# A four-segment memory attention and GEGLU layer on one core: masked keys written by small copies into zeroed tiles, free choice of PSUM pairs, and a replanned order

## The chip, the cores and the metric

One Trainium2 chip, one core of it. The metric is the device time of one execution in microseconds (us), lower is better. The kernel before takes 561.71 us, the median of three runs (561.22 to 561.72). Its engines are named as in the profile: PE multiplies matrices, PEld loads its weights, DVE and ACT and POOL work on tiles in SBUF (the on-chip memory) and in PSUM (eight banks, into which PE writes), SP issues nearly all DMAs.

## The reference, cut to what matters

The input has 2048 rows of 512. Two layers are applied twice with the same weights: an attention A and a gated feed-forward block B, each behind a layer norm and each added to its input.

```python
for s in range(4):                       # four segments of 512 rows, 32 heads of 16
    logits = einsum(qs, ks) * scale + mask          # causal inside the segment
    a_dot = softmax(logits) @ vs
    a_mem = (phi(qs) @ M) / (phi(qs) @ z + 1e-6)    # phi(t) = t+1 if t>0 else exp(t)
    o = g * a_mem + (1 - g) * a_dot
    M, z = M + phi(ks).T @ vs, z + phi(ks).sum()    # handed to the next segment
x = x + concat(o) @ wo
x = x + (gelu(n(x) @ w_gate) * (n(x) @ w_up)) @ w_down
```

All tensors are bf16; both layers run twice over the four segments, so that there are eight attention stages and eight feed-forward stages, numbered k = 0 to 7.

## The kernel before, in words

**Planner.** The program is written out by a planner in Python, `order`. It keeps a clock for each engine (`Clocks`, `Engine`), decides at each moment which piece of PE work comes next, and emits the instructions of all five engines in the order thus found. On the chip each engine runs its own instructions strictly in that order and waits at semaphores; the planned times are not there any more. An `Item` is a piece of PE work with a due number in stages (`k - qk_due` for the query and key products of stage k, and so on) and a readiness test; `Engine.post` queues work for another engine with a slack, and the job with the smallest ready time plus slack comes first. The numbers in `POLICY` are these due numbers, slacks and limits.

**Work of a stage.** `qk` and `v` make the products for queries, keys and values, each a chain of four 512-column matmuls into one PSUM bank, which DVE or ACT evicts (`evict`, L366 and L367). Queries, keys and masked keys are tiles of 4 blocks b by 512; a block holds eight heads in 128 partitions. Scores go in 40 rounds a stage (`score_round`, L793): four matmuls side by side, on four row groups of PE. A row group holds 32 partitions, two heads. For the first head of a pair (par = 0) the matmul takes the upper 16 rows of the key tile `kf` and of q. For the second (par = 1) it takes all 32 rows of `kB`, a copy of the keys with the first head's rows set to zero. `kB` comes from POOL: after a key block is evicted, `k_done` (L539) posts a multiplication of the block by `maskB`, a column of zeros and ones. `score` takes two rounds at a time into two pairs of banks, one `exp` of 128x1024 on ACT for each pair (L1199), then a causal mask on POOL (L1205), and later a flush (L809): the product with the values, turned and normalised on DVE (L824, L828, L832, L839).

**Pairs of banks.** In the kernel before a pair is banks 2p and 2p+1, read through the view `ps_pairs`. `pick` gives other work a bank whose neighbour is in use, if there is one, so that whole pairs stay free; `cap` limits how many pairs other work may have.

**Memory part.** `phi` takes exp on ACT (L596), min with 1 (L614, on DVE for stage 0, on POOL after), and add on DVE (L600); for keys the result is turned by a DMA transpose (`turn_later`, L342), `phik`. The rows of the norm, `xn` (L435, DVE), are turned in the same way into `xnT`, for the attention stages and most of the feed-forward ones. The scale `rs` of a norm is made on POOL (L418, L423).

**PE modes.** A matmul is done whole (128 weight columns), or in four column strips of 32 beside each other (`product`, L376 and L379), or, for scores, in row groups. Going from one form to another costs time on PE, which the planner counts as `SWITCH`. Where PE has nothing ready, the planner emits products of the constant tile `warm`, here called fillers.

**Queue of SP.** Loads of inputs and weights, transposes and stores are all issued by SP in one order. Weight pieces are posted with an earliest planned time, but on the chip SP issues them as soon as those ahead of them are issued. Stage 0 keeps its q, kf and kB in space of `wd_sb`, which is loaded later.

Of the kernel before, what the change touches and what calls it, by code (L numbers as in the profile page):

```python
# [18 lines left out]
P = 128  # L19
# [35 lines left out]
    flush_wait=-1.813, piece_slack=1.086, kb_slack=2.08, mem_slack=-2.073, margin=1.389, qk_due=0.513,  # L55
    e_q=-0.257, e_k=1.032, exp_slack=0.902, e_slack=10.959, phi_slack=4.283, gelu_slack=1.187, act_evict=3.627,
    first_evict=4.817, gate_step=0.01, up_due=0.388, up_step=0.027, down_due=2.499, down_step=0.058,
    upd_due=-0.151, v0_due=-1.527, x1_at=10.541, x2_at=16.065, x3_at=40.015, cut_slack=6.049, direct=1,
    gelu_tiles=3, kb_dve=0, phi_pool=1, rounds=2, early=1, starve=0.518, cap=4, fuse=1)


class Engine:
# [4 lines left out]
    def __init__(self, overlap=0.0):  # L67
        self.free, self.overlap, self.jobs, self.table = 0.0, overlap, [], "exp"
        self.only = None
# [17 lines left out]
    def serve(self, now):  # L87

        self.jobs = [j for j in self.jobs if not j[4]]
        jobs = [j for j in self.jobs if not self.only or j[3] in (None, self.only)]  # L90
        if not jobs:
            return False
        start = max(self.free, min(j[0] for j in jobs) + self.LATENCY)
        if start > now:
            return False
        job = min((j for j in jobs if j[0] + self.LATENCY <= start + 0.03), key=lambda j: j[0] + j[1])
        ready, _, steps, table, taken = job
        taken.append(1)
        self.jobs.remove(job)
        t = ready  # L100
        if table and table != self.table:
            self.free += 1.28
            self.table = table
        for cost, emit, told in steps:
            t = max(self.free, t + self.LATENCY) + cost
            self.free = t - self.overlap
            if emit:
                emit()
            if told:
                told(t)  # L110
        return True


class Clocks:
# [6 lines left out]
    def __init__(self):  # L121
        self.pe = 0.0
        self.mode = "whole"
        self.act, self.dve, self.pool, self.sp = Engine(0.09), Engine(0.07), Engine(), Engine()
        self.engines = (self.dve, self.act, self.pool, self.sp)
        self.later, self.seq, self.waiting = [], 0, []
        self.dma, self.fills, self.stalls = 0.0, [], []
        self.ev = {}
# [103 lines left out]
def order(pol, nc, cst, seg, wrk, psp, A_x, A_wq, A_wk, A_wv, A_wo, A_beta, B_x, B_w_gate, B_w_up, B_w_down, out):  # L232
# [34 lines left out]
    pieces = [(14.0, 512, lambda: load_x(2)), (27.0, 512, lambda: load_x(3))]  # L267
# [17 lines left out]
    nc.vector.memset(warm[:], 1.0)  # L285

    ps_all = psp.tile([P, BANKS, L], F32, tag="ps", bufs=1, name="ps")
    ps_pairs = ps_all[:].rearrange("p (a b) c -> p a (b c)", b=2)
# [20 lines left out]
    maskB = cst.tile([P, 1], F32, name="maskB")  # L309
    nc.vector.reduce_sum(out=maskB[:], in_=bd[:, 16:P:32], axis=mybir.AxisListType.X)  # L310
# [81 lines left out]
    class Norm:  # L392
# [46 lines left out]
        def row(self, j, i, ready):  # L439
            xn = Box(lambda: self.normed(j, i))  # L440

            def landed(t):
                xn_slots.back(i, t)
                self.left -= 1
                if not self.left:
                    ev[self.key] = t

            def told(t):
                if self.key in BY_PE:
                    items.append(self.turn_item(j, xn, t, landed))  # L450
# [4 lines left out]
            ck.dve.post(ready, self.slack, (0.46, xn, told))  # L455
# [34 lines left out]
    class Att:  # L490
# [12 lines left out]
        def add_items(self):  # L503
# [5 lines left out]
            def first():  # L509
                if k:  # L510
                    self.q, self.kf, self.kB = (seg.tile([P, KT, L], BF16, tag=f"{n}{k % SETS}", bufs=1, name=n)
                                                for n in ("q", "kf", "kB"))
# [22 lines left out]
            def k_done(b, ps, at=None):  # L535
                def told(t):
                    ev["k", k, b] = t
                    eng, job, cost = (nc.vector, ck.dve, 0.345) if k < pol.kb_dve else (nc.gpsimd, ck.pool, 1.566)
                    job.post(t, pol.kb_slack if k else NORMAL, (cost, lambda: eng.tensor_scalar(  # L539
                        out=self.kB[:, b, :], in0=self.kf[:, b, :], scalar1=maskB[:, 0:1], scalar2=None,  # L540
                        op0=ALU.mult), lambda t2: ev.update({("kB", k, b): t2})))
# [13 lines left out]
            def v(j):  # L555
# [4 lines left out]
                def done():  # L560
# [6 lines left out]
                            lambda: ck.has(("xnTa", k)) and (k <= SETS or ("flush", k - SETS, 3, 1) in ev),  # L567
# [17 lines left out]
        def phi(self, b, which, ready, slack):  # L585
            def take(i):
# [29 lines left out]
                def summed(t):  # L616
                    ck.dve.post(t, pol.phi_slack, (0.75 if which == "q" else 0.83, add, told))

                def made(t):
                    if self.k < pol.phi_pool:  # L620
                        ck.dve.post(t, pol.phi_slack, (0.32, cut(nc.vector), None),
                                    (0.75 if which == "q" else 0.83, add, told))
                    else:
                        ck.pool.post(t, pol.cut_slack, (1.566, cut(nc.gpsimd), summed))
# [154 lines left out]
        def score_round(self, t, places):  # L779
# [5 lines left out]
            for ki, q0, n, c0 in PIECES[i]:  # L785
                for j in range(4):
# [6 lines left out]
                    nc.tensor.matmul(ps_all[:, 2 * pair + unit // 2, o:o + n], lhsT=lhsT[rows, b, P * ki:P * ki + P],  # L793
# [3 lines left out]
        def flush_item(self, b, par, places, masked):  # L797
# [16 lines left out]
            def done():  # L814
# [35 lines left out]
                def put():  # L850
                    steps = [(0.706, back, None if self.s else there)]
                    if self.s:
                        steps.append((0.447, add, there))
# [3 lines left out]
                if par:  # L857
                    steps += [(0.355, inverse, None), (0.7, scale, kept)]
# [185 lines left out]
    first_scale(2, 4)  # L1044
    n0.first_xn = [n0.normed(0, 0), n0.normed(1, 1)]
# [24 lines left out]
    ck.pe, ck.act.free, ck.dve.free, ck.pool.free, ck.sp.free = 8.8, 9.45, 8.9, 6.2, 7.2  # L1070
# [4 lines left out]
    later_constants()  # L1075
    for at, kb, piece in pieces:
# [12 lines left out]
    norm_of_input(1, pol.x1_at, 0.5)  # L1089
    norm_of_input(2, pol.x2_at, 1.0)  # L1090
    norm_of_input(3, pol.x3_at, 1.0)
# [4 lines left out]
    score_pairs = set()  # L1096
# [14 lines left out]
    def free(bank, t):  # L1111
        return banks[bank] <= t
# [7 lines left out]
    def rounds_now():  # L1120

        if not streams:
            return 0
        ready = 0
        for k, t in streams[:pol.rounds]:
            if not att[k].score_ready(t):
                break
            ready += 1
        n = min(len(free_pairs()), len(slot_free), ready)
        if n >= 3 and len(streams) != 4:  # L1130
            return 3
        if n >= 2 and len(streams) != 3 and (streams[0][0] < pol.early or len(streams) in (2, 4) or backlog() < pol.starve):
# [3 lines left out]
    def pick():  # L1136

        got = [i for i in range(BANKS) if free(i, ck.pe)]
        mine = len({i // 2 for i in range(BANKS) if banks[i] > ck.pe and i // 2 not in score_pairs})
        half = [i for i in got if not free(i ^ 1, ck.pe)]  # L1140
        if half:
            return min(half, key=lambda i: (-banks[i ^ 1], banks[i]))
        if got and (mine < pol.cap or not streams):
            return max(got, key=lambda i: i)
        return None
# [8 lines left out]
    def score(n):  # L1154
        pairs = free_pairs()[:n]
# [26 lines left out]
        groups = [[p] for p in range(n)] if n == 2 or not pol.fuse else [[2], [0, 1]] if pol.fuse == 1 else [[0, 1], [2]]  # L1182
        for group in groups:
            jobs, parts = [], []
            for p in group:
                pair, slot = pairs[p], slots[p][1]
                score_pairs.add(pair)
                slot_users[slot] = len(users[p])
                banks[2 * pair] = banks[2 * pair + 1] = 1e9
# [8 lines left out]
            def exp(p0=p0, p1=p1, s0=s0, s1=s1):  # L1198
                nc.scalar.activation(  # L1199
                    out=pt_all[:, s0:s1 + 1:max(s1 - s0, 1), :, :].rearrange("p s u c -> p s (u c)"),  # L1200
                    in_=ps_pairs[:, p0:p1 + 1:max(p1 - p0, 1), :], func=ACT.Exp, scale=SCALE)
# [6 lines left out]
            def told(a, parts=parts, jobs=jobs):  # L1208
                for pair, _ in parts:
                    score_pairs.discard(pair)  # L1210
                    banks[2 * pair] = banks[2 * pair + 1] = a
# [19 lines left out]
    while streams or items or opened or ck.busy():  # L1231
# [16 lines left out]
        if bank is not None:  # L1248
# [6 lines left out]

            if streams:
# [65 lines left out]
```

## Time and profile before

| what | value |
|---|---|
| median of the runs | 561.71 us |
| the profiled execution, its own time | 561.81 us |
| its span on the core | 560.1 us |
| busy share of PE, DVE, ACT, POOL | 97%, 80%, 81%, 58% |
| granted clock of PE | full in all 40 slices |
| kB on POOL (L539), 32 instructions | 46.5 and 6.8 us |
| min with 1 on POOL (L614), 44 instructions | 66.9 us |
| causal masks on POOL (L1205), 320 instructions | 184.1 us |
| exp on ACT (L1199), 320 instructions | 309.7 us |
| packets of DMA queue q1 | 20.1% of 16 engines' span |

Busy time of an engine is the time in which one of its instructions ran. A matmul's recorded time is its way through PE, longer than the distance to the next one, so that a long row of matmuls is priced by its whole length divided by its count. An idle time is put down to the instruction that released it.

### The profile page before, as it was taken

To read this page: it belongs to the slowest core of one execution; us is meant where nothing else is said; L and a number is where in the kernel's file an instruction comes from. 1 tells how busy PE (TensorE), PEld (TensorE's weight loads), DVE (VectorE), ACT (ScalarE), POOL (GpSimd) and SP (SyncE) were. 2 spreads that over 40 slices of the span, in tenths; PEclk is the share of its full clock that TensorE was granted. 3 is DMA by queue.
4 is the path that set the end of the run, shared out by engine and by line. 5 is a ranking of instruction groups with operands and counts; after the bars stand their busy time and mean duration, and the time that the engine had idled before them with its cause. 6 is when DMAs were issued, how large, how long until landed. Compare 5 with 4: busy or idle time off the path is not lost.

```text
span 560.1 us, 21158 instructions
## 1 busy us (share of the span) xinstructions
PE 542.6 (97%) x9193; PEld 271.0 (48%) x9234; DVE 449.8 (80%) x821; ACT 450.9 (81%) x533; POOL 323.8 (58%) x438
## 2 busy tenths in 40 slices
PE   7999999999999999999999999999999999999997
PEld 3444454444445444444444444445445445555544
DVE  4999899979998699789698887988976877886332
ACT  5899999999798978999999699998899986730230
POOL 3699899278724997258881389835785344200000
PEclk9999999999999999999999999999999999999999
DMA  7155801600231023400321030210310004100001
GB/s 225 32 117 169 180 2 31 180 2 2 40 68 12 3 30 61 64 2 12 49 40 22 20 59 4 48 23 12 57 43 22 2 3 78 40 3 21 19 1 37
DMA packets 64925, 25.76 MB, mean 46 GB/s; under 512 B 54336, under 2 KB 64832, under 8 KB 64832
## 3 DMA queue, kind: packets, MB, share of 16 engines
q1 hardware_dynamic: 64400, 24.13, 20.1%
q8 instruction: 72, 1.18, 0.9%
q10 hardware_dynamic: 432, 0.27, 0.2%
q14 instruction: 21, 0.17, 0.1%
HBM read 9.71 MB, written 2.10 MB: 21 GB/s over the span
## 4 chain that ended last, share of the span: by engine, by line
PE 69%; DVE 20%; DMA 4%; issue 3%; ACT 2%; POOL 1%; SPq 0%; ACTq 0%; DVEq 0%
PE ps L376 37%; PE ps L379 19%; PE ps L793 6%; PE ps L809 4%; DVE st L405 3%; DVE xn L435 3%; DVE x_sb L879 2%; DVE byq L824 2%; DMA phik<-e 2%; ACT pt L1199 2%; DVE gel_sb L366 1%; DVE ab L832 1%; DMA wv_sb<-in_A_wv_dram 1%; DVE phiq L600 1%; PE ps L665 1%
## 5 line engine op out<-in xcount | busy, mean ns | idle before, releaser
L1199 ACT ACTIVATE pt<-ps 128x1024 bf16<-128x1024 f32 x320 | 309.7, 1026 | 36.3 <-PE ps L793 32.4
L1205 POOL TENSOR_SCALAR_AFFINE_SELECT pt<-pt 128x512 bf16<-128x512 bf16 (+1 forms) x320 | 184.1, 589 | 132.5 <-ACT pt L1199 131.7
L939 DVE TENSOR_TENSOR gel_sb<-gel_sb,ps 128x512 bf16<-128x512 bf16 x112 | 74.5, 683 | 28.4 <-PE ps L379 17.1
L376 PE MATMUL ps<-wd_sb,gel_sb 128*32 128x512 bf16 (+1 forms) x1296 | 75.2, 370 | 0.0
L614 POOL TENSOR_SCALAR e<-e 128x512 bf16<-128x512 bf16 x44 | 66.9, 1520 | 5.8 <-ACT e L596 4.5
L879 DVE TENSOR_TENSOR x_sb<-x_sb,ps 128x512 bf16<-128x512 bf16 (+1 forms) x68 | 43.2, 645 | 30.9 <-PE ps L376 17.0
L376 PE MATMUL ps<-xnT,wg_sb 128*32 128x512 bf16 x1056 | 64.4, 380 | 0.6 <-DVE gel_sb L366 0.4
L376 PE MATMUL ps<-xnT,wu_sb 128*32 128x512 bf16 x1128 | 64.8, 379 | 0.0
L824 DVE STREAM_TRANSPOSE byq<-ps 128x512 f32<-128x512 f32 x64 | 45.1, 706 | 13.4 <-PE ps L809 12.9
L539 POOL TENSOR_SCALAR kB<-kf,maskB 128x512 bf16<-128x512 bf16 x28 | 46.5, 1661 | 8.5 <-DVE kf L366 8.0
L366 DVE CAST gel_sb<-ps 128x512 bf16<-128x512 f32 x57 | 38.1, 680 | 12.8 <-PE ps L376 5.9
L376 PEld LDWEIGHTS <-gel_sb 128*32 128x32 bf16 x1296 | 32.8, 96 | 29.2 <-issue 5.6
L376 PEld LDWEIGHTS <-wu_sb 128*32 128x32 bf16 x1128 | 30.3, 97 | 28.6 <-issue 2.4
L991 ACT ACTIVATE gel_sb<-gel_sb 128x1536 bf16<-128x1536 bf16 (+1 forms) x35 | 43.4, 1304 | 0.1
L379 PE MATMUL ps<-xnT,wg_sb 128*128 128x512 bf16 x170 | 41.9, 379 | 1.1 <-issue 0.5
L809 PE MATMUL ps<-pt,vaug 128*32 128x256 bf16 (+1 forms) x1344 | 40.8, 256 | 0.0
L405 DVE BATCH_NORM_STATS2 st<-x_sb 128x6 f32<-128x512 bf16 x60 | 40.5, 675 | 0.4
L376 PEld LDWEIGHTS <-wg_sb 128*32 128x32 bf16 x1056 | 27.1, 96 | 26.1 <-issue 5.7
L379 PE MATMUL ps<-xnT,wu_sb 128*128 128x512 bf16 x157 | 37.1, 379 | 0.8 <-issue 0.5
L435 DVE TENSOR_SCALAR xn<-x_sb,mv,rs 128x512 bf16<-128x512 bf16 x64 | 34.2, 592 | 2.7 <-POOL rs L423 2.2
L809 PEld LDWEIGHTS <-vaug 128*32 128x32 bf16 x1344 | 30.5, 97 | 11.4 <-issue 3.9
L793 PE MATMUL ps<-q,kf 16*128 16x256 bf16 (+1 forms) x672 | 31.1, 255 | 1.9 <-ACT pt L1199 1.3
(129 smaller groups left out, 757.2 us busy)
## 6 DMA issues: line engine op xcount, KB each, us to landing
wg_sb<-in_B_w_gate_dram SPq DMA_DIRECT2D x8, 224.0 KB, 5.1
wu_sb<-in_B_w_up_dram SPq DMA_DIRECT2D x8, 224.0 KB, 4.4
wd_sb<-in_B_w_down_dram SPq DMA_DIRECT2D x7, 256.0 KB, 3.1
x_sb<-in_A_x_dram SPq DMA_DIRECT2D x3, 512.0 KB, 6.8
out_dram<-x_sb SPq DMA_DIRECT2D x12, 128.0 KB, 1.7
xnT<-xn SPq DMA_TRANSPOSE x48, 2.5
wv_sb<-in_A_wv_dram SPq DMA_DIRECT2D x1, 512.0 KB, 6.9
wo_sb<-in_A_wo_dram SPq DMA_DIRECT2D x4, 128.0 KB, 3.0
```

The source lines that it names most:

```text
L376: nc.tensor.matmul(out[r], lhsT=lhsT[:, r], rhs=rhs, start=start, stop=stop, tile_position=(0, 32 * c))
L379: nc.tensor.matmul(out, lhsT=lhsT, rhs=rhs, start=start, stop=stop)
L405: nc.vector.bn_stats(out=self.st6[:, 0, :], in_=x_sb[:, self.tt0 + j, :])
L435: nc.vector.tensor_scalar(out=xn[:], in0=x_sb[:, self.tt0 + j, :], scalar1=self.mv[:, j, 0:1], scalar2=self.rs[:, j, :], op0=ALU.subtract, ...
L614: return lambda: eng.tensor_scalar(out=e[0][:], in0=e[0][:], scalar1=1.0, scalar2=None, op0=ALU.min)
L793: nc.tensor.matmul(ps_all[:, 2 * pair + unit // 2, o:o + n], lhsT=lhsT[rows, b, P * ki:P * ki + P], rhs=self.q[rows, b, q0:q0 + n], start= ...
L809: nc.tensor.matmul(ps()[32 * j:32 * j + 32, q0:q0 + n], lhsT=self.vaug[:, ki, h * (DH + 1):h * (DH + 1) + 32], rhs=pt_all[:, slot, unit, c ...
L824: nc.vector.transpose(out=self.byq[:, par, :, :].rearrange("p a c -> p (a c)"), in_=ps()[:])
L879: ck.dve.post(ck.made(), slack, (0.15 + 0.00104 * (c1 - c0), lambda: nc.vector.tensor_tensor(out=xt, in0=xt, in1=ps()[:, 0:c1 - c0], op=AL ...
L939: ck.dve.post(ck.made(), NORMAL, (0.683, lambda: nc.vector.tensor_tensor(out=g, in0=g, in1=ps()[:], op=ALU.mult), lambda t: (ps.read(t), e ...
L1199: nc.scalar.activation(out=pt_all[:, s0:s1 + 1:max(s1 - s0, 1), :, :].rearrange("p s u c -> p s (u c)"), in_=ps_pairs[:, p0:p1 + 1:max(p1 ...
L1205: nc.gpsimd.affine_select(out=half, in_=half, pattern=[[0, w], [1, P]], compare_op=ALU.is_ge, fill=0.0, base=0, channel_multiplier=-1)
```

## The change

Masked keys are no longer made by POOL. Three constant tiles `kBs` (and stage 0's space in `wd_sb`) are set to zero once at the start, and after each eviction of a key block four DMAs, issued by SP, copy the 16 rows of the second head of each row group out of `kf`. That is 4 x 32 = 128 DMAs of 16 rows of 1 KB. `maskB` and its reduction are gone. A pair of score banks may be any two neighbours (`pairs_of`). The min with 1 of stage 0 goes from DVE to POOL as well (`phi_pool=0`). The planner counts DVE and POOL as slower where they overlap (`Slowed`), loads the third segment's input at the start and the fourth's at a planned time, lets no value product of stage 0 begin before 12.4 us of planned time, changes the rules for when scores, other work and fillers are emitted (`rounds_now`, `pick`, `backlog`), and has new `POLICY` numbers. The arithmetic of all other operations is as before.

```diff
-    eng, job, cost = (nc.vector, ck.dve, 0.345) if k < pol.kb_dve else (nc.gpsimd, ck.pool, 1.566)
-    job.post(t, pol.kb_slack if k else NORMAL, (cost, lambda: eng.tensor_scalar(
-        out=self.kB[:, b, :], in0=self.kf[:, b, :], scalar1=maskB[:, 0:1], scalar2=None,
-        op0=ALU.mult), lambda t2: ev.update({("kB", k, b): t2})))
+    for j in range(4):
+        r = slice(32 * j + DH, 32 * j + 2 * DH)
+        ck.sp.post(t, pol.kb_slack if k else URGENT, (0.62, lambda r=r: nc.sync.dma_start(
+            out=self.kB[r, b, :], in_=self.kf[r, b, :]), kb_sent if j == 3 else None))
...
+    nc.vector.memset(wd_sb[:, 2 * KT:3 * KT, :], 0.0)
+    kBs = [cst.tile([P, KT, L], BF16, name=f"kB{i}") for i in range(SETS)]
+    nc.gpsimd.memset(kBs[1][:], 0.0)
+    for n, kB in enumerate((kBs[2], kBs[0])):
+        ck.pool.post(15.0 + 8.0 * n, 4.0, (1.85, lambda kB=kB: nc.gpsimd.memset(kB[:], 0.0), None))
...
-    lambda: ck.has(("xnTa", k)) and (k <= SETS or ("flush", k - SETS, 3, 1) in ev),
+    lambda: ck.has(("xnTa", k)) and (k or ck.pe > 12.4) and (k <= SETS or ("flush", k - SETS, 3, 1) in ev),
...
-    return [p for p in range(BANKS // 2) if free(2 * p, ck.pe - 0.05) and free(2 * p + 1, ck.pe - 0.05)]
+    return pairs_of({i for i in range(BANKS) if banks[i] <= ck.pe - 0.05})
...
-    in_=ps_pairs[:, p0:p1 + 1:max(p1 - p0, 1), :], func=ACT.Exp, scale=SCALE)
+    in_=ps_all[:, p0[0]:p0[1] + 1, :], func=ACT.Exp, scale=SCALE)
...
+    mine = sum(banks[i] > ck.pe for i in range(BANKS) if i not in score_banks)
+    if streams and mine >= pol.cap and backlog() < pol.near and rounds_ready(2):
+        return None
```

Policy numbers that stand out: `qk_due` 0.513 to 1.423 (query and key products are due earlier by nine tenths of a stage), `phi_pool` 1 to 0, `exp_slack` 0.902 to -11.449, `act_evict` 3.627 to 6.014, `x3_at` 40.0 to 9.0.

More of the change, by code (lines that the diff above doesn't have):

```diff
@@ L1109, in next_e, with pairs_of, rounds_ready, rounds_now @@
             ck.serve()
[L1111 to L1112 removed]
+    def pairs_of(got):
+        pairs, i = [], 0
+        while i < BANKS - 1:
+            if i in got and i + 1 in got:
+                pairs.append((i, i + 1))
+                i += 1
+            i += 1
+        return pairs
     def free_pairs():
[L1115 removed]
+        return pairs_of({i for i in range(BANKS) if banks[i] <= ck.pe - 0.05})
     def backlog():
         return max(ck.act.free, ck.pe) - ck.pe + sum(j[2][0][0] for j in ck.act.jobs if not j[4] and j[3] == "exp")
[L1120 to L1130 removed]
+    def rounds_ready(n):
+        for k, t in streams[:n]:
+            if not att[k].score_ready(t):
+                return False
+        return len(streams) >= n and len(slot_free) >= n
+    def rounds_now(idle=False):
+        if not streams or not rounds_ready(2):
+            return 0
+        n, left = len(free_pairs()), len(streams)
+        wait = backlog()
+        if pol.rounds > 2 and n >= 3 and left != 4 and wait < pol.ahead and rounds_ready(3):
             return 3
[L1132 removed]
+        if n >= 2 and left != 3 and (idle or left in (2, 4) or wait < (pol.early if streams[0][0] < 1 else pol.starve)):
             return 2
@@ L1136, in pick @@
     def pick():
[L1138 to L1145, printed above, removed]
+        got = [i for i in range(BANKS) if banks[i] <= ck.pe]
+        if not got:
+            return None
+        mine = sum(banks[i] > ck.pe for i in range(BANKS) if i not in score_banks)
+        if streams and mine >= pol.cap and backlog() < pol.near and rounds_ready(2):
+            return None
+        apart = {i for i in range(BANKS) if i not in score_banks and banks[i] > ck.pe + pol.soon} if streams else ()
+        return min(got, key=lambda i: (-len(pairs_of(set(range(BANKS)) - {i, *apart})), banks[i]))
     def open_item(got, bank):
@@ L1154, in score @@
     def score(n):
[L1155 removed]
+        pairs = sorted(free_pairs(), key=lambda p: max(banks[p[0]], banks[p[1]]))[:n]
         slots = sorted([slot_free.pop(0) for _ in range(n)], key=lambda x: x[1])
@@ L1181, in score @@
         ck.on_pe(0.107 * n + 0.015)
-        groups = [[p] for p in range(n)] if n == 2 or not pol.fuse else [[2], [0, 1]] if pol.fuse == 1 else [[0, 1], [2]]
+        groups = [[p] for p in range(n)]
         for group in groups:
@@ L1254, in order @@
                 continue
+        n = rounds_now(True)
+        if n:
+            score(n)
+            continue
+        if bank is not None:
             if streams:
```

82 lines of the change are left out of this document (51 added, 31 removed).

## Prediction

> **What bounds the kernel now.** I read the shares on the page first, then the four engines' busy time in stretches of the span, then the first 20 us instruction by instruction, then the groups of the operations that the change touches, and last the chain of waits.
>
> ```profile
> PE 542.6 (97%) x9193; PEld 271.0 (48%) x9234; DVE 449.8 (80%) x821; ACT 450.9 (81%) x533; POOL 323.8 (58%) x438
> PEclk9999999999999999999999999999999999999999
> ```
>
> The clock is full throughout. PE is busy for 97%, so a change can take time out only where PE idles, where it does fillers, or where it changes its form. The stretches (a busy time and a count for PE, PEld, DVE, ACT, POOL) tell where:
>
> ```profile
> 0.00:20.00 20.00, 16.04 (x144) 7.40 (x145) 11.89 (x36) 12.36 (x21) 7.88 (x19) 1.00 0.51 159
> 20.00:60.00 40.00, 38.54 (x783) 18.41 (x781) 37.91 (x76) 37.77 (x47) 39.10 (x50) 1.00 0.50 119
> 12.50:150.00 137.50, 135.03 (x2332) 66.05 (x2346) 126.72 (x245) 126.95 (x155) 112.55 (x143) 1.00 0.31 75
> 150.00:482.00 332.00, 324.20 (x5992) 160.39 (x6017) 277.22 (x490) 297.06 (x340) 204.40 (x280) 1.00 0.19 34
> 482.00:560.10 78.10, 74.75 (x823) 40.34 (x816) 40.12 (x68) 19.68 (x27) 2.04 (x4) 1.00 0.05 15
> ```
>
> From 20 to 60 us all four are full (PE 38.5, DVE 37.9, ACT 37.8, POOL 39.1 of 40 us): part of what PE does there are fillers, because it waits for the others. After 150 us DVE, ACT and POOL have room (83%, 89%, 62%), and PE idles for 332 - 324.2 = 7.8 us. The last 78 us are feed-forward work after the last score; the change does not touch them. The start:
>
> ```profile
> 12.49 1.67 PE L379 MATMUL ps<-wv_sb,xnT 128*128 128x512 bf16 x6 [2.00 <-DMA wv_sb<-in_A_wv_dram]
> 13.62 0.69 DVE L366 CAST gel_sb<-ps 128x512 bf16<-128x512 f32 x1 [3.47 <-PE ps L379]
> ```
>
> PE stands 2.00 us for the value weights, and DVE 3.47 us for the first value product.
>
> **PE's own work.** The order of PE's instructions in both kernels can be counted without a time. The products are the same. Scores go in 160 groups of two rounds in both, so that the freer pairs give no larger groups. Fillers: 80 strips and 6 whole become 88 and 6, which is 26 and 28 products of 512 columns. Changes between whole, strips and row groups: 353 become 344. Prices from three rows:
>
> ```profile
> 102.66 1.04 PE L376 MATMUL ps<-warm 128*32 128x512 bf16 x16
> 103.63 0.40 PE L793 MATMUL ps<-q,kf 16*128 16x256 bf16 x8
> 103.96 1.25 PE L379 MATMUL ps<-xnT,wu_sb 128*128 128x512 bf16 x4
> ```
>
> In a long row of strips, 528 instructions of the chain take 28.52 us, so a product (four strips) takes 0.216 us. Four fillers from 102.66 end at 103.52 and the scores start at 103.63: a change costs 0.11. The sum is 2 x 0.216 - 9 x 0.11 = **-0.56 us**.
>
> **kB leaves POOL.** The groups:
>
> ```profile
> L614 POOL TENSOR_SCALAR e<-e 128x512 bf16<-128x512 bf16 x44 | 66.9, 1520 | 5.8 <-ACT e L596 4.5
> L539 POOL TENSOR_SCALAR kB<-kf,maskB 128x512 bf16<-128x512 bf16 x28 | 46.5, 1661 | 8.5 <-DVE kf L366 8.0
> L435 DVE TENSOR_SCALAR xn<-x_sb,mv,rs x64: 372/688/823, 6.2 to 511.1; 128x512 bf16<-128x512 bf16 x64
> ```
>
> POOL loses 46.5 us and stage 0's 6.8 (4 of 1.70), 53.3 in all. It gains 4 minima of 1.52 = 6.1 and three memsets of 128x2048. The trace has one of 128x128 bf16 at 0.20 and tiny ones at 0.10, so a memset of 16 times the size lies between 1.6 and 3.2; I take 2.0, 6 us. One stands after the two `rs` of the start (6.37 + 0.80), while POOL idles up to 10.79; the second stands before the `rs` of segment 1 and can delay it by up to 2 us. Net -41 us on POOL. This is worth something only through what waited behind POOL. DVE's memset of stage 0's kB lies in its idle time before 3.49 us and costs nothing; the reduction of `maskB` (0.16) goes from the same gap.
>
> DVE loses 4 minima of 0.34. Its order holds 13 more evictions at 0.68 (+8.8), ACT's 13 fewer at 0.61 (-7.9): a shift to the engine with more room after 150 us. DVE also shares something with POOL: `xn` takes 372 ns at least, 688 in the median. If all above 372 came from POOL, that is 64 x (592 - 372) = 14 us at the mean of the page's group, and with 41 of 324 us of POOL gone, an eighth or **1.8 us** goes; below nothing is excluded, as nothing here adds POOL work overall. The Trainium skill ("SBUF — State Buffer", Who interferes with whom) has it that the one which issues first holds the shared ports for its whole instruction and the other is fully blocked. By that rule an `xn` behind a fresh 1.66 us `kB` could take 0.37 + 1.66 = 2.0; the longest of 64 is 0.82, so the trace does not bear it out, and the sum would be some 4 us lower by it.
>
> **kB goes to SP.** SP issues 128 more DMAs. Two loads issued together took 1.05 us, so one costs about 0.53, 68 us in all, on a queue that carries 96 transposes at 1.22 (117 us). SP has room on average. A block's copies take 4 x 0.53 issue, and landing was 1.6 us for stores of 64 KB and 2.5 for a transpose: 3.2 to 4.1 us from the eviction, against 1.66 plus POOL's queue. A block's first kB round comes five rounds after its first kf round, and two rounds are two exps of 1.03, so five are 5.1 us of ACT: in a running stage the copies are hidden. They cost if a block is evicted under 4.1 us ahead of its kB rounds. Stage 0 is the tight place: kf is evicted at 10.69 (10.20 + 0.49), the copies land by 10.69 + 2.1 + 1.6 = 14.4, or 17.2 if each landing is as slow as the 4.9 us of the 8 KB of beta amid the loads. Up to its third group of scores PE has 5.5 us of work after the first at 10.09, so 15.6. The cost is 0 to 1.6 us; I take 0.
>
> **The start.** The first value products now stand behind the other query and key products, whose weights were landed at 9.5 us (issued 3.72, 5.8 to land). PE's 2.00 us and DVE's 3.47 us of waiting go. But ten more fillers (2.2 us) stand before segment 1's first product (22 strip fillers there against 12, and 6 whole in both), so PE itself gains nothing before that; eight fillers' worth (1.7 us) goes at later places. What the start gives is a lead for DVE and ACT in the stretch where all are full. To score group 48 (about 141 us) ACT's order holds 3.3 us less than before; to the 18th flush turn DVE's holds 0.9 less, and it starts 3.5 earlier; PE's holds 0.6 less, and 2.0 of waiting is gone. The least of the three gains rules: **-2.6 us** (between 0, if PE only gets fillers, and -5, if DVE had been the limit).
>
> **After 150 us.** The 7.8 us of PE idling has chains through POOL ahead of it in three places:
>
> ```profile
> 145.99 1.49 POOL e L614
> 147.87 1.34 POOL rs L423
> ...
> 201.62 1.34 POOL rs L423
> 203.40 2.05 DVE xn L435 x3
> ...
> 212.56 4.87 DMA phik<-e
> ...
> 286.41 0.89 POOL e L614
> 287.92 1.32 POOL pt L1205 x2
> ...
> 297.60 3.13 DMA phik<-e
> ```
>
> POOL becomes shorter by 1.66 us wherever a kB stood in front, the queries and keys come earlier, but every other place of the order is new. Bounds: all of it gone (-7.8), or as much again (+7.8). I take a third gone, **-2.5 us**, the share that stands behind POOL. The -0.56 is contained in the -0.6 of PE's order above, so it is not added again.
>
> **Sum.** 561.81 - 2.6 - 2.5 = **556.7 us** against the profiled execution's own time (span 560.1 and 1.7 around it), which lies 0.1 above the median of the runs. I predict **556.6 us**.
>
> **Rivals.** *More goes (551):* the start gives the whole lead of DVE (-5) and two thirds of the later idling go (-5.3). For it: POOL stood at 39.1 of 40 us. Against: PE, not DVE, sets the pace after 150 us, and only three chains show POOL. Chance 0.22, of which 0.03 is for the case that an `xn` meeting a kB waits for its end (half of 1.66 us instead of 0.22, about 4 us over the kernel), which is the page's rule above. *SP becomes the wait (566):* SP issues in order, and the order has five blocks of 16 kB copies ahead of `phik`, `xnT` or `amT` transposes. A copy waits for its key block's eviction, and each transpose behind it waits too; a full block is 16 x 0.53 = 8.5 us. `phik` is in the chain already (4.87 and 3.13 us). If a quarter of the block, 2.1 us, reaches PE at each of five places, +10.5 outweighs the -5.1, some 567; it decides once a transpose is due within 8.5 us of the last key eviction. Against: keys are now due nine tenths of a stage earlier. Chance 0.20. *It doesn't do what it says (561.7):* kB was never waited for by PE, and the new order's stalls replace the old. For it: no wait of PE on L539 is among the listed. Chance 0.10. The Trainium skill ("DMA: Bandwidth & Descriptors", Rules for kernel authors) advises against many small transfers: under 64 KB one pays mostly overhead. No row has a 16 KB copy inside SBUF; the 64 KB stores at 1.6 us give the bound above.
>
> **The numbers.** My forecast has 0.48, around 556.6 (553 to 560). The range reaches over most of the first two rivals, 550 to 566. A measurement tells 0.2% (1.1 us) from no change; the forecast gives 0.04 of its chance to that. Faster 0.67, same 0.12, slower 0.21.
>
> **What would show it.** Right: PE's wait for the value weights gone, POOL busy near 283 us, `xn` under 592 ns in the mean, PE idling under 7.8 us between 150 and the last score, kB landing within 4.1 us. Wrong: PE or ACT released by kB or by a transpose that SP issued late; new waits of PE after 150 us.

## The result and the profile after

The changed kernel takes 563.16 us, the median of eight runs (562.91 to 565.34); the kernel before took 561.57 beside it, the median of eight (561.16 to 562.11). The ratio is **1.0037, 95% interval 1.0024 to 1.0049**: slower by 0.37%, where 556.6 was forecast; the time lies between that and the 566 of the rival *SP becomes the wait*.

| | before | after |
|---|---|---|
| the profiled execution, its own time | 561.81 us | 563.01 us |
| its span | 560.1 us | 561.3 us |
| start of the last group of scores on PE | 479.90 us | 484.68 us |
| from there to the end of the span | 80.2 us | 76.6 us |

From the page of the changed kernel, engines' busy time and granted clock:

```profile
PE 547.3 (98%) x9251; PEld 270.5 (48%) x9251; DVE 454.3 (81%) x830; ACT 445.1 (79%) x520; POOL 284.9 (51%) x413
PEclk9989999999999999999999999999999999999999
```

POOL fell from 323.8 to 284.9 us, so the work went where the change says. New is the 8 in the clock's third slice (28 to 42 us). Next the busy times by stretches of the changed kernel (columns as in the prediction: start and end, length, then PE, PEld, DVE, ACT, POOL; then the granted clock):

```profile
0.00:20.00 20.00, 16.64 (x141) 7.49 (x145) 14.41 (x37) 12.99 (x22) 10.14 (x21) 1.00 0.54 165
20.00:60.00 40.00, 37.12 (x682) 17.40 (x678) 32.50 (x65) 32.73 (x40) 26.77 (x40) 0.96 0.53 114
12.50:150.00 137.50, 131.89 (x2278) 63.80 (x2277) 119.28 (x230) 121.78 (x144) 90.29 (x127) 0.99 0.35 81
150.00:486.00 336.00, 334.13 (x6143) 164.79 (x6144) 289.42 (x517) 296.67 (x337) 187.25 (x270) 1.00 0.21 37
486.00:561.30 75.30, 72.16 (x780) 37.45 (x772) 37.69 (x65) 20.95 (x29) 2.54 (x4) 1.00 0.05 15
```

The two halves of the span went opposite ways. **After 150 us** PE idles 336.00 - 334.13 = 1.9 us, where it had idled 7.8. **Before 150 us** it idles 137.50 - 131.89 = 5.6, where it had idled 2.5, and part of its busy time is at a lower clock. From 20 to 60 us no engine is full any more: POOL went from 39.1 to 26.8 us, but DVE and ACT too from 37.9 and 37.8 to 32.5 and 32.7. All of them wait, and the timelines say for what. First the start:

```profile
6.31 0.73 DVE L452 TENSOR_SCALAR xn<-x_sb,mv,rs 128x512 bf16<-128x512 bf16 x2
7.23 1.80 POOL L1067 MEMSET kB<- 128x2048 bf16 x1
7.31 2.18 DVE L452 TENSOR_SCALAR xn<-x_sb,mv,rs 128x512 bf16<-128x512 bf16 x2 [0.21 <-POOL rs L1045]
9.23 0.71 PE L494 MATMUL ps<-ident,xn 128*128 128x128 bf16 x8 [1.74 <-DVE xn L452]
11.65 0.40 PE L815 MATMUL ps<-wd_sb 16*128 16x256 bf16 x8
```

Two `xn` take 0.73 us together at 6.31; the two at 7.31, which start 0.08 us behind POOL's new memset, take 2.18. PE waits 1.74 us for them, and the first scores start at 11.65 instead of 10.09. Then segment 1, SP's queue and what PE does with it:

```profile
24.07 3.09 SPq L359 DMA_TRANSPOSE xnT<-xn  x2
27.22 0.76 SPq L267 DMA_DIRECT2D x_sb<-in_A_x_dram  x1
28.08 8.88 SPq L359 DMA_TRANSPOSE xnT<-xn  x6
```

```profile
34.49 1.07 PE L393 MATMUL ps<-xnT,wq_sb 128*32 128x512 bf16 x16 [2.39 <-DMA xnT<-xn]
```

The fourth segment's input, 512 KB that take 7.1 us to land, is issued between two transposes. The chain of waits gives 5.08 us from 29.37 to the landing of a transpose behind it, against a median of 2.5, and PE stands for 2.39 us. The stretches around this wait, in the changed kernel:

```profile
28.00:35.00 7.00, 4.61 (x74) 1.90 (x70) 3.29 (x8) 5.62 (x6) 5.46 (x9) 1.00 1.05 153
35.00:42.00 7.00, 7.00 (x140) 3.37 (x132) 4.94 (x12) 4.34 (x6) 1.69 (x4) 0.76 0.28 62
```

Right behind the wait the granted clock is 0.76 in the mean of 7 us (the record has 0.5 for 3.41 us). Then SP's queue ahead of segment 2; the eighteen rows left out are more of such copies and weight loads, with hardly a break between them:

```profile
39.55 0.53 SPq L562 DMA_DIRECT2D kB<-kf  x1
40.13 1.54 SPq L267 DMA_DIRECT2D wo_sb<-in_A_wo_dram  x1
...
55.29 1.63 SPq L562 DMA_DIRECT2D kB<-kf  x2
57.36 0.34 SPq L267 DMA_DIRECT2D wg_sb<-in_B_w_gate_dram  x1
57.81 1.23 SPq L359 DMA_TRANSPOSE phik<-e  x1
59.16 4.97 SPq L359 DMA_TRANSPOSE xnT<-xn  x3
```

The 16 copies of segment 1 and 11 weight loads fill SP from 39.55 to 57.7 us; the copies' rows add up to 9.4 us, 0.59 each. DVE has made the `xn` of segment 2 by 53.5 us (four at 51.36, 2.13 us), and their transposes are issued at 59.16, 5.7 us later. The last place is the same queue when segment 2's keys are copied: DVE has made the input of a `phik` transpose by 70.93 us (70.25 + 0.68), and SP issues it 13.0 us later, behind two other `phik`, 12 copies and weight loads. From the timeline of all engines:

```profile
70.25 0.68 DVE L622 SCALAR_TENSOR_TENSOR e<-wd_sb,e 128x512 bf16<-128x512 bf16 x1
...
74.37 3.22 SPq L562 DMA_DIRECT2D kB<-kf  x4
...
78.26 2.42 SPq L562 DMA_DIRECT2D kB<-kf  x4
...
81.41 2.41 SPq L562 DMA_DIRECT2D kB<-kf  x4
...
83.92 1.76 SPq L359 DMA_TRANSPOSE phik<-e  x1
```

PE waits at both places, 0.62 us for segment 2's `xnT` and 1.08 us for this `phik`:

```profile
67.71 1.02 PE L396 MATMUL ps<-xnT,wq_sb 128*128 128x512 bf16 x4 [0.62 <-DMA xnT<-xn]
...
86.86 0.97 PE L741 MATMUL ps<-gel_sb,phik 128*128 128x128 bf16 x13 [1.08 <-DMA phik<-e]
```

### The profile page after: what moved, and what is told of

Read it like the earlier page. It is cut to its first block, busy times and chain, and to the rows that moved or that the text cites. A ratio compares the mean times of both kernels' runs of the same rounds, so it can differ in the third digit from the quotient of the medians.

```text
span 561.3 us, 21400 instructions
## 1 busy us (share of the span) xinstructions
PE 547.3 (98%) x9251; PEld 270.5 (48%) x9251; DVE 454.3 (81%) x830; ACT 445.1 (79%) x520; POOL 284.9 (51%) x413
## 4 chain that ended last, share of the span: by engine, by line
PE 75%; DVE 17%; DMA 3%; issue 3%; POOL 1%; ACT 1%; DVEq 0%; POOLq 0%
PE ps L393 40%; PE ps L396 21%; PE ps L815 7%; PE ps L831 5%; DVE xn L452 2%; DVE st L422 2%; DVE byq L846 2%; DVE x_sb L901 2%; DMA xnT<-xn 1%; DVE e L622 1%; PE ps L741 1%; DVE aT L861 1%; DVE ab L854 1%; DVE gel_sb L383 1%; PE ps L687 1%
## 5 line engine op out<-in xcount | busy, mean ns | idle before, releaser
L636 POOL TENSOR_SCALAR e<-e 128x512 bf16<-128x512 bf16 x48 | 74.2, 1548 | 8.5 <-ACT e L618 6.2
L393 PE MATMUL ps<-xnT,wg_sb 128*32 128x512 bf16 x1172 | 71.3, 380 | 0.3 <-DVE gel_sb L383 0.3
L393 PE MATMUL ps<-xnT,wu_sb 128*32 128x512 bf16 x1164 | 66.7, 379 | 0.0
L393 PE MATMUL ps<-wd_sb,gel_sb 128*32 128x512 bf16 (+1 forms) x1088 | 62.4, 369 | 0.0
L396 PE MATMUL ps<-wd_sb,gel_sb 128*128 128x512 bf16 (+1 forms) x232 | 43.7, 340 | 0.0
L393 PEld LDWEIGHTS <-wg_sb 128*32 128x32 bf16 x1172 | 29.0, 96 | 29.3 <-issue 6.6
L393 PEld LDWEIGHTS <-gel_sb 128*32 128x32 bf16 x1088 | 26.8, 96 | 24.7 <-issue 4.8
L396 PE MATMUL ps<-xnT,wg_sb 128*128 128x512 bf16 x155 | 36.7, 379 | 0.6 <-DVE byq L846 0.4
L452 DVE TENSOR_SCALAR xn<-x_sb,mv,rs 128x512 bf16<-128x512 bf16 x64 | 32.2, 559 | 5.8 <-DMA xnT<-xn 3.6
L815 PE MATMUL ps<-q,kB 32*128 32x256 bf16 (+1 forms) x672 | 31.4, 254 | 0.3 <-DVE xnT L383 0.2
```

Source lines behind the costliest of these rows:

```text
L393: nc.tensor.matmul(out[r], lhsT=lhsT[:, r], rhs=rhs, start=start, stop=stop, tile_position=(0, 32 * c))
L396: nc.tensor.matmul(out, lhsT=lhsT, rhs=rhs, start=start, stop=stop)
L636: return lambda: eng.tensor_scalar(out=e[0][:], in0=e[0][:], scalar1=1.0, scalar2=None, op0=ALU.min)
L815: nc.tensor.matmul(ps_all[:, pair[unit // 2], o:o + n], lhsT=lhsT[rows, b, P * ki:P * ki + P], rhs=self.q[rows, b, q0:q0 + n], start=True, ...
```

## The experiments

The first theory (e1 to e4) had two losses, the memset beside `xn` and the load between the transposes, with a stretch at half the clock as a price on top of a long wait. SP's full queue was added as a third when e3, with both mended, missed the 557.5 to 559 that was expected. The rivals: that kB by copies is itself too slow or too dear, and that the new order after 100 us is at fault. All kernels but e4 keep the changed kernel's order on PE, DVE and ACT (e7 adds one reduction, e10 its products), so that the start of the n-th group of scores on PE can be compared one by one. From the traces, in us:

| kernel | 1st | 11th | 23rd | 33rd | 160th (last) |
|---|---|---|---|---|---|
| changed | 11.65 | 40.20 | 69.53 | 97.84 | 484.68 |
| e1, memset early | 10.26 | 39.18 | 68.55 | 99.11 | 486.15 |
| e2, load early | 11.82 | 36.22 | 69.15 | 97.78 | 484.67 |
| e3, both | 10.08 | 35.04 | 67.41 | 95.52 | 482.41 |
| e9, copies in pairs | 11.57 | 38.64 | 67.19 | 93.79 | 480.61 |
| e6, all three | 10.23 | 34.63 | 63.18 | 89.78 | 476.71 |

From the 33rd group to the last, all six take 386.8 to 387.0 us. Whatever tells them apart happens before 100 us. The order behind is not at fault: between the same two groups the kernel before takes 387.0 us (92.87 to 479.90), and from the last group to the end it takes 80.2 us against 76.6.

### e1: the memset moved ahead of the norms

```diff
+    nc.gpsimd.memset(kBs[1][:], 0.0)      # right behind kBs = [...]
...
-    nc.gpsimd.memset(kBs[1][:], 0.0)      # behind the two rs
```

> The changed kernel, with the first of POOL's three memsets moved ahead of the start's two norm scales, into POOL's idle time before 5.4 us; every other instruction keeps its place. Theory (three parts: the memset at 7.23 us holds up DVE's xn, the load of the fourth segment's input holds up the transposes of xnT, and the rest of the change gains about 4 us): xn at 7.31 falls from 1.88 to about 0.4 us, the first scores stand at 10.1 instead of 11.65, but PE still waits for xnT near 34 us, so that at most 1.5 us comes off, and perhaps nothing until the load is moved: 561.5 to 563. Rival (the xn was late for another reason, such as its scale or its input): xn stays at 1.9 us and the time at 563.2.

Measured: 564.0 us, ratio to before 1.0034 (1.0017 to 1.0050), above what was expected. PE's timeline of e1:

```profile
10.26 0.40 PE L816 MATMUL ps<-wd_sb 16*128 16x256 bf16 x8
...
33.47 1.46 PE L394 MATMUL ps<-xnT,wq_sb 128*32 128x512 bf16 x16 [2.75 <-DMA xnT<-xn]
```

The first scores come 1.39 us earlier, as a loss at the memset must give, but PE then waits 2.75 us for the same transposes, the clock falls again, and the last group comes 1.5 us later than in the changed kernel, most of that lost between the 23rd and the 33rd, where PE waits again, 1.44 us of it for `phik`; the two medians are not told apart. The cause is shown, its price in the total is hidden by the next one.

### e2: the load moved ahead of the transposes

```diff
     load_x(2)
+    load_x(3)
...
-    ck.sp.post(pol.x3_load, pol.piece_slack, (0.57, lambda: load_x(3), last_input))
+    ck.sp.post(pol.x3_load, pol.piece_slack, (0.57, None, last_input))
```

> The changed kernel, with the load of the fourth segment's input issued at the start, right behind that of the third, and taken out from between the transposes of segment 1; nothing else moved. Theory: the transposes land some 3 us after issue instead of 5 to 6, PE's wait of 2.4 us for xnT goes, and the dip of the granted clock that follows it (0.76 in 35 to 42 us) goes with it: 563.2 - 2.4 - 1 to 1.7 = 559 to 560. Rival A (SP's 16 copies of stage 0 make the transposes late): first transpose still at 24.1 us, PE's wait stays over 1.5 us, 562 to 563. Rival B (start is bound by DVE's order anyway): 563.

Measured: 562.2 us, ratio 1.0005 (0.9992 to 1.0018), not the 559 to 560 expected. The wait at 34 us is gone and the 11th group starts 4.0 us earlier. At the 23rd all but 0.4 of it is lost; PE's timeline of e2, then its stretch behind it:

```profile
66.03 1.49 PE L397 MATMUL ps<-xnT,wq_sb 128*128 128x512 bf16 x4 [2.90 <-DMA xnT<-xn]
```

```profile
66.00:70.00 4.00, 3.98 (x24) 1.26 (x28) 0.75 (x2) 0.74 (x2) 0.00 (x0) 0.57 0.58 183
```

PE, now ahead, waits 2.90 us for segment 2's `xnT`, and again a stretch at half the clock follows. By the ratios e2 is 0.3% faster than the changed kernel; the profiled execution (562.99 us) is one of the slower of its eleven.

### e3: both

> Both edits together. Theory: 563.2 - 1.5 - 3.5 = 557.5 to 559, which is the forecast for the change within 2 us; faster than the kernel before by 0.5 to 0.7%. Rival A or B: not under 561.

Measured: 561.12 us, ratio 0.9985 (0.9973 to 0.9996). Of the 5.2 us won by the 11th group, 2.1 are left at the 23rd. SP's timeline of e3 shows where it stops:

```profile
54.15 1.23 SPq L361 DMA_TRANSPOSE phik<-e  x1
55.49 4.91 SPq L361 DMA_TRANSPOSE xnT<-xn  x3
...
61.13 1.19 SPq L361 DMA_TRANSPOSE xnT<-xn  x1
```

DVE had those `xn` at 48.35 us (46.21 + 2.14), 7.1 us ahead of the first issue. PE stands for 2.0 us until 63.95, and a stretch at half the clock follows again. With the start mended, SP's queue is what the kernel waits for. The profile puts PE's 2.0 us down to an eviction by DVE that ends at the same moment (63.26 + 0.65); e5 and e6 change only SP's issues, and this wait is gone from both.

### e4: the copies in the order of before

The kernel before with kB made in the new way: memsets, and four copies on SP in the place of POOL's multiplication. The third segment's input is also loaded at the start, as in the changed kernel; the diff below leaves this out.

```diff
-                    job.post(t, pol.kb_slack if k else NORMAL, (cost, lambda: eng.tensor_scalar(
-                        out=self.kB[:, b, :], in0=self.kf[:, b, :], scalar1=maskB[:, 0:1], ...
+                    def copies():
+                        for j in range(4):
+                            r = slice(32 * j + DH, 32 * j + 2 * DH)
+                            nc.sync.dma_start(out=self.kB[r, b, :], in_=self.kf[r, b, :])
```

> The kernel before, in its own order on PE, DVE and ACT, with only the masked keys made by four DMAs each instead of by POOL (zeroed tiles, memsets in idle time; SP issues the copies where POOL's instruction stood in the order). Theory (copies are harmless and relieve POOL, the loss is at the start of the new order): POOL loses 53 us, xn falls under 0.57 us in the mean, the old order cannot use much of it: 559.5 to 561.5. Rival (128 copies on SP are what costs): transposes behind copies land late, PE waits for them, 563 to 566.

Measured: 580.17 us, ratio 1.0325 (1.0308 to 1.0341), far outside both expectations. The longest of PE's waits in e4 (total, times, longest), and a part of SP's timeline ahead of the longest:

```profile
PE ps L379 <- DMA xnT<-xn: 17.1, 2, 12.6
```

```profile
74.40 1.21 SPq L345 DMA_TRANSPOSE xnT<-xn  x1
75.71 2.43 SPq L545 DMA_DIRECT2D kB<-kf  x4
78.24 1.21 SPq L345 DMA_TRANSPOSE xnT<-xn  x1
```

In an order that was not planned for them the copies stand between the transposes of `xnT`, and one wait is 12.6 us. The granted clock is at 0.5 for 20.5 us in all, so the time holds more than the waits. This is the rival *SP becomes the wait* at its full size; the changed kernel's new order avoids most of it, not all.

### e5: fewer weight loads (from e3)

The twelve loads of `wo` and `w_gate` become three larger ones, issued ahead of segment 1's copies.

```diff
+    def load_ahead():
+        load(w_att["o"][:], w_view(A_wo))
+        for h in range(2):
+            r = slice(2 * h, 2 * h + 2)
+            load(wg_sb[:, r, :], w_view(B_w_gate)[:, r, :])
```

> The version with both start edits, and the 12 loads of wo and w_gate that stand between the kB copies of stage 1 merged into 3, issued ahead of these copies: SP issues 9 DMAs (some 5.4 us) less before segment 2's transposes. Nothing moves on PE, DVE, ACT and POOL. Theory (SP is issuing without a break from 34.8 to 62 us, so that segment 2's xn, ready at 48.0, is turned only from 55.5; PE waits 2.2 us at 61.6 and then runs 3.41 us at half clock): the transposes start some 5 us earlier, the wait and the slow stretch go, 561.1 - 2.2 - 1.7 = 557 to 558, PE's clock 1.0 throughout. Rival (PE waits there for something other than SP, or the merged loads hold the transposes up in the DMA queues): 560.5 to 562.

Measured: 558.61 us, ratio 0.9947 (0.9932 to 0.9961), where e3 had 0.9985. PE's waits of e5 no longer name `xnT`; the largest left is another transpose:

```profile
PE ps L750 <- DMA phik<-e: 1.5, 1, 1.5
```

That is the later of the two places. The merged loads have cleared the queue ahead of segment 2's `xnT`, not behind it, where the copies still stand in front of a `phik`, issued at 77.91.

### e6: two blocks to a copy (from e3)

From stage 1 on, a copy waits for two blocks of keys and takes both, 32 KB: 72 copies instead of 128.

```diff
+                        b2 = slice(b - 1, b + 1) if k else slice(b, b + 1)
-                        ck.sp.post(..., (0.62, lambda r=r: nc.sync.dma_start(
-                            out=self.kB[r, b, :], in_=self.kf[r, b, :]), ...
+                        ck.sp.post(..., (0.62, None if k and b % 2 == 0 else (
+                            lambda r=r, b2=b2: nc.sync.dma_start(out=self.kB[r, b2, :], in_=self.kf[r, b2, :])), ...
```

> The version with both start edits, and from stage 1 on each copy of masked keys covers two blocks (32 KB), issued after the second of them is evicted: 72 copies instead of 128, 56 issues of about 0.6 us less on SP, of which 8 (4.8 us) before segment 2's transposes. Theory (SP's issue time is the cost, not the bytes): the same gain as by merging loads, 557 to 558.5. Rival A (PE waits for kB, which is up to half a stage later now): PE waits on kB, 561 or more. Rival B (SP is not what PE waits for): 561.

Measured: **554.95 us**, ratio 0.9887 (0.9874 to 0.9899): 1.1% under the kernel before, the fastest of all. SP's timeline of e6, and its stretches:

```profile
48.99 2.02 SPq L361 DMA_TRANSPOSE phik<-e  x1
51.12 3.82 SPq L361 DMA_TRANSPOSE xnT<-xn  x3
```

```profile
12.50:150.00 137.50, 135.10 (x2405) 66.40 (x2407) 126.09 (x245) 127.18 (x152) 97.03 (x134) 1.00 0.34 82
150.00:479.00 329.00, 325.65 (x5996) 161.53 (x6020) 282.43 (x502) 290.39 (x329) 180.35 (x263) 1.00 0.21 37
```

The transposes are issued 4.4 us ahead of e3's (51.12 against 55.49), the clock is full, and PE idles 2.4 us from 12.5 to 150. A copy of 32 KB lands in 2.3 us where one of 16 KB took 1.8, so half the issues cost little in landing. The expectation had the same gain for e5 and e6. Their 23rd groups do start together (63.21 and 63.18), but the 33rd starts 2.2 us earlier in e6 (89.78 against 91.94): the pairs empty the queue at the later place too, and PE no longer waits for the `phik` there.

### e7: kB on POOL again, in the new order (from e3)

> The version with both start edits, with the masked keys made by POOL again, one instruction where the first of a block's four copies stood in the order; SP has no copies left. Theory (the copies do relieve POOL and DVE, and cost only through SP's queue): SP's wait goes, so segment 2's transposes are early, but POOL has 53 us more, full again from 20 to 100 us, masks and norm scales late, xn back to 0.59 us: 560 to 564. Rival (what POOL gives up is worth nothing, and only the new order and the free pairs gain): 557 to 558.5, as with the merged loads.

Measured: 572.26 us, ratio 1.0189 (1.0173 to 1.0204). A stretch and PE's longest group of waits in e7:

```profile
20.00:100.00 80.00, 70.24 (x1279) 34.67 (x1277) 64.31 (x122) 64.21 (x78) 73.53 (x91) 0.96 0.36 81
```

```profile
PE ps L836 <- POOL pt L1250: 9.7, 8, 3.3
```

POOL is full (73.5 of 80 us), and PE waits 9.7 us for values whose causal masks stand behind kB. That is 8 us above the range expected. In this order, which was planned for them, the copies are worth some 11 us (572.26 here, 561.12 in e3); 6.83 us at half the clock behind one of the waits are part of it. Here, then, taking kB from POOL is sound. With e4 this shows that neither half of the change gains alone: the copies lose in the old order, and the new order loses with kB on POOL.

### e8: e5 and e6 together

> Both start edits, loads merged and copies in pairs: SP issues 17 DMAs less before segment 2's transposes. Theory: once the transposes are no longer late there is no more to gain there, 556.5 to 558, and not over 1 us faster than with one of the two edits alone. Rival (every SP issue costs, everywhere): clearly faster than either, 555 or less.

Measured: 555.24 us, ratio 0.9897 (0.9883 to 0.9911), not told apart from e6, as the theory had it, though both lie under its 556.5. Once SP's queue has room, more room is worth nothing.

### e9: pairs alone, on the changed kernel

The edit of e6, with the memset and the load left as the change has them.

> The changed kernel with kB copied two blocks at a time from stage 1 on, and the start left as the change has it (memset of the first kB behind the two rs, fourth segment's input at its planned place). Theory (two separate losses, the start and SP's order, which add up): the start's 5.15 us stay lost, so 555.0 + 5.1 = 560.1 us, with the wait of 2.4 us for xnT at 34 and half the clock from 35 to 39 still there, and none at 61 to 68. Rival (the start's loss is only visible because SP's queue is late behind it; with a free queue it is made up): about 555 to 556.

Measured: 558.93 us, ratio 0.9958 (0.9939 to 0.9977). SP's timeline, PE's timeline and the stretches of e9:

```profile
51.95 4.57 SPq L359 DMA_TRANSPOSE xnT<-xn  x3
```

```profile
34.51 1.05 PE L393 MATMUL ps<-xnT,wq_sb 128*32 128x512 bf16 x16 [2.48 <-DMA xnT<-xn]
```

```profile
35.00:42.00 7.00, 7.00 (x157) 3.59 (x150) 6.44 (x14) 5.54 (x7) 3.26 (x6) 1.00 0.61 150
```

DVE has segment 2's `xn` at 51.94 us (49.81 + 2.13), and SP issues the transposes at once, not 5.7 us later. Against e6 the groups are 4.0 us late at the 11th and 3.9 at the last: the start's loss is carried to the end undiminished, so the rival (it would be made up) falls. But the clock stayed full here behind a wait of 2.48 us, against what was expected: a wait of that length does not always bring the half clock (the last section says what tells the two apart). Setting it beside the changed kernel gives the price of the stretch at that point: nearly the same wait, same start (11.57 and 11.65), and the 11th group 1.56 us later where the clock fell; in the 7 us behind it PE issued 140 matmuls instead of 157. Of e9's seven executions, the five at a mean clock of 1.0 took 557.89 to 558.95 us, the two at 0.996 and 0.997 took 560.97 and 560.95.

### e10: the wait filled with products (from e9)

```diff
+                    for _ in range(9):
+                        for c in range(4):
+                            r = slice(32 * c, 32 * c + 32)
+                            nc.tensor.matmul(ps()[r], lhsT=warm[:, r], rhs=wide, start=True, stop=True,
+                                             tile_position=(0, 32 * c))
```

> The same, with nine more products of warm (36 strips, 9 x 0.216 = 1.94 us) on PE ahead of the first query product of segment 1, that is inside its wait for xnT at 32 to 34.5 us; nothing else moves. They do no useful work. Theory (the stretch at half the clock follows from PE standing still for over 2 us, and costs half of 3.41 = 1.7 us): PE waits about 0.45 us, the clock stays at 1.0 from 35 to 42, and the time is 1.7 us under that of the kernel without them. Rival (the clock falls for another reason, or its cost is hidden because DVE and ACT set the pace from 35 to 60 us): the same time, or up to 1.9 us more where the products do not fit into the wait.

Measured: 559.6 us, ratio 0.9960 (0.9944 to 0.9975), not told apart from e9 (0.9958). The wait at 34 us is filled, but this settles nothing about the clock, since e9's profile shows none of the stretch that the filling was to avoid. In e10's own profile the clock fell elsewhere; a stretch of it:

```profile
10.00:14.00 4.00, 4.00 (x28) 1.95 (x26) 1.16 (x5) 1.66 (x4) 0.00 (x0) 0.58 0.67 226
```

That is behind PE's 1.74 us wait for the `xn` held by the memset, a wait that the changed kernel and e9 have as well, with the clock full behind it.

## Why the prediction was wrong

**The sum.** Taking e6 as the change without its losses, the changed kernel loses 484.68 - 476.71 = 8.0 us before 100 us: 3.9 at the start (e6 against e9), and 4.1 by SP's queue and the clock (e9 against the changed kernel). In the two profiled executions the 4.1 are 1.56 up to the 11th group, by the clock, 0.8 more up to the 23rd, where PE waits for `xnT`, and 1.7 up to the 33rd, where it waits for `phik`. These three do not simply add: executions of the changed kernel at a mean clock of 1.0 took 562.91 to 563.23 us, no less than the profiled one at 0.997 (563.01). Presumably what a full clock wins is waited away at SP's queue, as e2's lead was. Against before, e6 is faster by 1.1%, 6.3 us, where the forecast had 5.1. The gain that was forecast is there; three costs set at nothing or left out ate it.

**"One stands after the two `rs` of the start, while POOL idles"** failed. The memset was sized well (2.0 forecast, 1.80 measured) and did cost POOL nothing. It cost DVE: the `xn` that met it took 1.87 us, to the memset's end and a little beyond, and e1 gives the price at the first scores, 1.39 us. The prediction had the Trainium skill's rule for it ("SBUF — State Buffer", Who interferes with whom: whoever issues first keeps the shared ports for its whole instruction) and set it aside because no `xn` of 64 took over 0.82 us. Those 64 rows held no memset of POOL. For a memset the trace agrees with the rule: 2.18 us for two against 0.73. The trace also shows that not every DVE instruction is held: beside the memset at 27.63 (1.80 us) a multiplication of DVE (L854, f32 input) takes its usual 0.69.

**"The start: -2.6 us"** failed in sign. PE's wait for the value weights is gone, as forecast. But the step counted the work in DVE's, ACT's and PE's order and not what SP issues: the moved load stands ahead of two transposes that segment 1 needs, and it slows their landing from 2.5 to 5.08 us. By e2 it costs 4.0 us at the 11th group: 2.4 of wait and 1.56 of clock.

**"kB goes to SP ... SP has room on average"** is the step that failed most widely. Issue (0.53 forecast, 0.59 measured) and landing (1.6 to 2.5 forecast, 1.8 measured) were right, and so was stage 0 at nothing. What was wrong is the average: from 39.5 to 57.7 us SP has no room, and its order puts 16 copies ahead of transposes that were ready; from 74.4 to 83.9 it puts 12 ahead of a `phik`. It is the rival *SP becomes the wait* by its own mechanism, "a transpose due within 8.5 us of the last key eviction", at two places instead of five. Its price by e9 is 0.8 and 1.7, some 2.5 us in these executions.

**After 150 us, -2.5** was right in kind and too small. Idling fell from 7.8 to 1.9 us. Part of the 7.8 is not idling: e6 runs this part in the changed kernel's time, yet its rows show 329.00 - 325.65 = 3.35 us idle with 24 matmuls missing from the record (5996 against 6020 weight loads), and before's rows lack 25. So some 1.5 of before's 7.8 is missing records, and the gain is an estimated 4.4 us. With -4.4 there, the start's -2.6 as forecast, which no run measures by itself, and the 8.0 lost, the sum is +1.0; the profiled executions differ by +1.2. That "the change does not touch" the work behind the last score was wrong: it takes 76.6 us instead of 80.2, with 824 matmuls instead of 860, so the new order has moved some of it ahead.

**POOL and `xn`** came out near: 284.9 us against 283, and a mean under 592 ns. From the page of the changed kernel (busy, mean; for DMAs, KB and us to landing):

```profile
L636 POOL TENSOR_SCALAR e<-e 128x512 bf16<-128x512 bf16 x48 | 74.2, 1548 | 8.5 <-ACT e L618 6.2
...
L452 DVE TENSOR_SCALAR xn<-x_sb,mv,rs 128x512 bf16<-128x512 bf16 x64 | 32.2, 559 | 5.8 <-DMA xnT<-xn 3.6
...
kB<-kf SPq DMA_DIRECT2D x112, 16.0 KB, 1.8
```

`xn` took 2.1 us less in all (64 x (592 - 559) ns), where 1.8 was forecast, and that with the 1.5 lost at the memset inside it.

## What to carry to other kernels

Work moved from a full engine to a DMA queue is paid in issue slots, in order: count the issues in the stretch ahead of each transfer that somebody waits for, not over the span, and make each issue carry more. A single mended wait shows little in the total when the next late transfer is close behind; mend all of the chain, then take them away one by one. When a rule is rejected by a trace, ask whether the trace holds the operation that the change adds.

## What the runs showed of the hardware

The granted clock falls to 0.5 for 3.41 us, or a multiple of it, after PE has stood still, and not in every run: eight runs of the changed kernel had a mean clock of 1.0 three times and 0.996 or 0.997 five times. A wait of 2.39 us brought it in one profile and one of 2.48 in another did not, and 1.74 us brought it once. The Trainium skill ("TensorE: Matmul & The Clock Gate", Part 1: The HAM clock gate) has a free-running window of 3413 ns, with which the length and the difference between runs agree; its advice to keep gaps under some 3 us (same page, Why this matters for your kernels) is too generous here, as the 1.74 and 2.39 us show.

How much of a window must be idle can be read from the traces. In every trace the stretches at full clock between the first record and the last are whole multiples of 3.413 us too (9 and 153 of them in the changed kernel), so the borders of the windows can be counted on from one change of the clock to the next. The 2.39 us lay inside one window, 31.98 to 35.40 us. The 2.48 of e9, from 32.03 to 34.51, was split by a border at 33.16 (5.86 + 8 x 3.413) into 1.13 and 1.35, and the clock stayed full. Over the twelve traces, each window at full clock in which PE idled for 2.02 us or more was followed by half the clock (2.02, 2.04, 2.10, 2.39, 2.51, 2.75 and 2.90 us, in e7, e4, e3, the changed kernel, e4, e1 and e2), and of those with 1.91 or less only e10's with 1.74, while 1.91 in e7 and 1.74 in e9 were not. Why e10's was stays open. By these traces a wait costs the clock where some 2 us of it fall into one window, and where the borders lie differs from execution to execution.
